# Where the weights of a fused attention and softplus-MoE kernel are converted, and which engine makes its first x tiles

## The chip, the cores and the metric

The kernel runs on one core of a Trainium2 chip. The metric is the device time of one execution in microseconds (us). Five engines work side by side, each through its own instructions in order: TensorE (PE, matmuls; its weight loads are PEld), VectorE (DVE), ScalarE (ACT), GpSimd (POOL) and SyncE (SP), which here issues nearly all DMAs.

## The reference

Attention with rotary embedding over 4 batches of 8 heads (S = 576, D = 64), and its output, laid out as 2304 tokens of 512, through one expert with softplus:

```python
q_rot, k_rot = rotate(q), rotate(k)
scores = (1 / sqrt(D)) * matmul(q_rot, k_rot.T)
scores = scores - max(scores, axis=-1)
attn = exp(scores); attn = attn / (sum(attn, axis=-1) + 1e-9)
x = matmul(attn, v)                      # -> (2304, 512)
h = x @ w_in                             # 512 -> 2048
g = maximum(h, 0) + log1p(exp(-abs(h)))
out = g @ w_out                          # 2048 -> 512
```

## The kernel before

**Precision.** Every matmul runs on pairs of fp32r numbers: an operand is a high part and a low part (the rest), and three products are added. The weights w_in and w_out arrive as 64-bit floats and are turned into such pairs on the chip, by `conv_w`. For one chunk of columns it loads the raw words (`wraw`, L98, SP) and then makes six steps: the upper word scaled on ACT (L115), masked and shifted on DVE (L117) while ACT converts the lower word (L119), the sign merged on DVE (L121), the two added on DVE (L124), the high part wh cast on ACT (L127), the low part wl subtracted on DVE (L129). The generator yields between the steps, so that whoever drives it decides between which other instructions a step stands. The weights of one f (128 of the 2048 inner columns) are 512 columns of w_in and 512 of w_out.

**Attention loop.** It has 160 items, five 128-wide score chunks for each of 32 heads, and 171 slots, s = 0 to 170. In slot s the scores of item s are made on PE (L322) into the one buffer of their kind, and DVE reduces them to a row maximum (mx, L324). Nine slots later the item is made again transposed (L359), ACT takes two exponentials (L365, L366), DVE their difference (pl, L373), and two slots after that PE multiplies with v (pv, L391). `shift1` splits a head's maxima on GpSimd (shl, L270 and L273), and the shift goes into the stacked q. GpSimd also makes most of the rope (L273) and the low part of v (L297). q and k of a head are stacked by DMA (qs, L304 and L305; ks, L306 and L307) out of raw pairs (L260). Finished heads go through `evac` (xt, L399) to DRAM (xd L403, row sums xs L404); when a batch is done, `recip` makes 1/sum on DVE (L413, L414) and writes it to rd.

**MoE.** x comes back from DRAM in tiles of 384 tokens, four chunks of 128 rows each (`load_x`, L154 and L157: one load of xd, two of rd, twice that where a tile reaches over two batches). `split_x` multiplies by 1/sum (L162, GpSimd), rounds to the high part (L165, GpSimd) and subtracts for the low part (L166). There are 96 units, a tile and an f each: `emit_h` makes h (12 matmuls, L173), its softplus through e (DVE L183), ACT L185, m (DVE L188) and the pair g (ACT L190, DVE L193); `emit_o` multiplies with w_out (9 matmuls, L209). h runs two units ahead of o. Units begin with f below SEG for tiles 0 and 1 in turn, then tile 2, then the rest.

**What sets the order.** Nearly all compute instructions are pinned in program order (`pin`, `keep`); DMAs without `pin` are placed by a scheduler. `conv` makes f = 0 and 1 in eight chunks of 256 columns, one step in every third slot from 9 to 159. `late` makes the other f in two generators, w_in and w_out in turn, which `convert` drives: six calls in slots 163 to 168, and then three calls within each unit from the third on; the first six calls drive only the first generator, later ones both, and every sixth call does nothing. x of tiles 0 and 1 is loaded in slots 151 to 158 and split in slots 162 to 169, the low part on DVE. x of tile 2 is loaded and split among the first units.

## Time and profile before

| | |
|---|---|
| runs of the kernel before | median 764.06 us of 3 (762.26 to 764.2) |
| the profiled execution's own time | 763.71 us |
| its span | 761.9 us |
| PE busy | 728.3 us, 96% of the span |
| DVE busy | 520.7 us, 68% |
| ACT busy | 387.2 us, 51% |
| POOL busy | 311.1 us, 41% |
| mean granted clock of PE | 0.982 |

The span runs from the first to the last instruction that the profiler sees. PE is busy nearly throughout. The other engines are much less so, but each of them works beside PE through queues in order, so what matters is the few places where PE waits for one, and a busy PE can hide a short wait, since the ends of its matmuls are modelled.

### The profile page before, as it was taken

To read this page: it belongs to the slowest core of one execution; us is meant where nothing else is said; L and a number is where in the kernel's file an instruction comes from. 1 tells how busy PE (TensorE), PEld (TensorE's weight loads), DVE (VectorE), ACT (ScalarE), POOL (GpSimd) and SP (SyncE) were. 2 spreads that over 40 slices of the span, in tenths; PEclk is the share of its full clock that TensorE was granted. 3 is DMA by queue.
4 is the path that set the end of the run, shared out by engine and by line. 5 is a ranking of instruction groups with operands and counts; after the bars stand their busy time and mean duration, and the time that the engine had idled before them with its cause. 6 is when DMAs were issued, how large, how long until landed. Compare 5 with 4: busy or idle time off the path is not lost.

```text
span 761.9 us, 11924 instructions
## 1 busy us (share of the span) xinstructions
PE 728.3 (96%) x4288; PEld 670.8 (88%) x4288; DVE 520.7 (68%) x812; ACT 387.2 (51%) x730; POOL 311.1 (41%) x376
## 2 busy tenths in 40 slices
PE   5589999999999999998999999999999999999998
PEld 5479999999989999997888989899999989899996
DVE  6468888888888788878988888874353344444343
ACT  1057777777777777675566555532222222222221
POOL 6248888888888888337500000060190000000000
PEclk9589999999999999999999999999999999999999
DMA  6967776877778776743433333232040001001001
GB/s 188 237 154 206 197 206 173 225 196 206 188 204 220 199 189 157 178 142 99 119 108 111 112 111 111 97 118 71 1 145 1 1 1 42 1 1 43 0 1 42
DMA packets 49515, 91.41 MB, mean 120 GB/s; under 512 B 7248, under 2 KB 19856, under 8 KB 49456
## 3 DMA queue, kind: packets, MB, share of 16 engines
q1 hardware_dynamic: 46480, 85.77, 41.8%
q10 hardware_dynamic: 2976, 4.88, 1.7%
q8 instruction: 34, 0.56, 0.3%
q14 instruction: 25, 0.20, 0.1%
HBM read 51.00 MB, written 9.58 MB: 80 GB/s over the span
## 4 chain that ended last, share of the span: by engine, by line
PE 82%; DVE 8%; DMA 4%; issue 2%; POOL 1%; ACT 1%; SPq 1%; POOLq 0%; ACTq 0%; DVEq 0%
PE hp L173 24%; PE pv L391 13%; PE oa L209 12%; PE ob L209 12%; PE sp L322 10%; PE sp L359 10%; DVE mx L324 2%; DMA ks<-raw 2%; DMA qs<-raw 1%; DVE raw L273 1%; DVE pl L373 1%; POOL xraw L162 1%; DMA tab<-cs 1%; DVE g L193 1%; DVE wc L121 1%
## 5 line engine op out<-in xcount | busy, mean ns | idle before, releaser
L173 PE MATMUL hp<-xhl,wh 128*128 128x384 f32 x768 | 196.4, 336 | 0.6 <-DVE m L188 0.6
L324 DVE TENSOR_REDUCE mx<-sp 128x1 f32<-128x576 f32 x160 | 120.9, 755 | 63.5 <-PE sp L322 62.9
L185 ACT ACTIVATE e<-e 128x384 f32<-128x384 f32 x96 | 50.4, 525 | 199.2 <-DVE e L183 189.7
L173 PEld LDWEIGHTS hp<-xhl,wh 128*128 128x128 f32 x768 | 140.5, 188 | 9.5 <-DVE m L188 0.9
L322 PE MATMUL sp<-ks,qs 128*128 128x288 f32 x640 | 119.9, 311 | 22.9 <-DVE mx L324 11.6
L365 ACT ACTIVATE ph<-sp 128x576 fp32r<-128x576 f32 x160 | 103.8, 649 | 59.2 <-PE sp L359 58.9
L173 PE MATMUL hp<-xhl,wl 128*128 128x384 f32 x384 | 129.5, 337 | 0.8 <-DVE wl L129 0.7
L322 PEld LDWEIGHTS sp<-ks,qs 128*128 128x128 f32 x640 | 96.2, 196 | 31.0 <-DVE mx L324 18.7
L359 PE MATMUL sp<-qs,ks 128*128 128x288 f32 x640 | 116.1, 304 | 0.0
L391 PE MATMUL pv<-ph,vs 128*64 128x288 f32 (+1 forms) x640 | 112.2, 297 | 3.0 <-DVE xt L399 2.0
L183 DVE TENSOR_SCALAR e<-hp 128x384 int32<-128x384 int32 x96 | 53.4, 556 | 83.4 <-PE hp L173 83.1
L366 ACT ACTIVATE sp<-sp 128x576 f32<-128x576 f32 x160 | 102.9, 643 | 0.0
L359 PEld LDWEIGHTS sp<-qs,ks 128*128 128x128 f32 x640 | 93.7, 190 | 6.8 <-DVE pl L373 4.7
L209 PE MATMUL oa<-wh,g 128*128 128x512 f32 x288 | 97.7, 393 | 0.0
L373 DVE TENSOR_TENSOR pl<-sp,ph 128x576 fp32r<-128x576 f32 x128 | 95.8, 749 | 2.2 <-ACT sp L366 1.3
L209 PE MATMUL ob<-wh,g 128*128 128x512 f32 x288 | 97.3, 393 | 0.0
L391 PEld LDWEIGHTS pv<-ph,vs 128*64 128x64 f32 (+1 forms) x640 | 84.2, 161 | 5.8 <-ACT ph L365 2.2
L273 POOL TENSOR_TENSOR raw<-raw,tab 128x576 f32<-128x576 f32 x58 | 84.4, 1475 | 9.2 <-DMA raw<-qk 9.2
L193 DVE TENSOR_TENSOR g<-m,g 128x384 fp32r<-128x384 f32 x96 | 59.2, 616 | 37.7 <-ACT g L190 37.4
L273 POOL TENSOR_TENSOR raw<-raw 128x576 f32<-128x576 f32 (+1 forms) x56 | 80.6, 1439 | 3.7 <-ACT raw L267 1.5
L188 DVE SCALAR_TENSOR_TENSOR m<-hp,e 128x384 f32<-128x384 f32 x96 | 53.4, 556 | 41.1 <-ACT e L185 40.4
L190 ACT CAST g<-m 128x384 fp32r<-128x384 f32 x96 | 49.2, 513 | 50.4 <-DVE m L188 46.8
(72 smaller groups left out, 901.7 us busy)
## 6 DMA issues: line engine op xcount, KB each, us to landing
raw<-qk SPq DMA_DIRECT2D x32, 576.0 KB
wraw<-w SPq DMA_DIRECT2D x28, 512.0 KB
ks<-raw SPq DMA_DIRECT2D x32, 320.0 KB
qs<-raw SPq DMA_DIRECT2D x32, 288.0 KB
ks<-raw SPq DMA_DIRECT2D x32, 160.0 KB
vf<-v SPq DMA_DIRECT2D x32, 160.0 KB
qs<-raw SPq DMA_DIRECT2D x32, 144.0 KB
xd<-xt SPq DMA_DIRECT2D x32, 144.0 KB
```

The source lines that it names most:

```text
L173: pin(nc.tensor.matmul(out=hp, lhsT=a[f][:, c * 128:(c + 1) * 128], rhs=pieces[j, c][:, b, :], start=(i == 0), stop=(i == 11),))
L183: pin(nc.vector.tensor_single_scalar(out=e.bitcast(I32), in_=hp.bitcast(I32), scalar=-(2 ** 31), op=ALU.bitwise_or))
L193: pin(nc.vector.tensor_tensor(out=g[:, 1, :], in0=m, in1=g[:, 0, :].bitcast(F32), op=ALU.subtract))
L209: pin(nc.tensor.matmul(out=po, lhsT=g[:, s, t * 128:(t + 1) * 128], rhs=b[f][:, 512:1024], start=(first and i == 0), stop=(last and i == 2),))
L273: pin((nc.vector if e == "V" else nc.gpsimd).tensor_tensor(out=out, in0=in0, in1=in1, op=op))
L322: pin(nc.tensor.matmul(out=sp[:, j, :HS], lhsT=q[:, i, cq], rhs=k[:, 0, ck], start=(i == 0), stop=(i == 1)))
L324: pin(nc.vector.tensor_reduce(out=mx_t[h][:, c:c + 1], in_=sp[:, :, :HS], axis=AX.XY, op=ALU.max, negate=True))
L359: pin(nc.tensor.matmul(out=sp[:, i, :HS], lhsT=k[:, j, ck], rhs=q[:, j, hs], start=(j == 0), stop=(j == 1)))
L365: pin(nc.scalar.activation(out=ph, in_=sp, func=AF.Exp, scale=D ** -0.5))
L366: pin(nc.scalar.activation(out=sp, in_=sp, func=AF.Exp, scale=D ** -0.5))
L373: pin(nc.vector.tensor_tensor(out=pl, in0=sp[:, :, :HS], in1=ph.bitcast(F32), op=ALU.subtract))
L391: pin(nc.tensor.matmul(out=pv[rows, i, :HS], lhsT=lhs, rhs=rhs[:, i, :], start=(c == 0 and j == 0), stop=(c == 4 and j == len(terms) - 1)))
```

## The change

FC goes from 2 to 1: `conv` makes only f = 0, in two chunks of 512 columns, with both loads issued at the very start and its steps in slots 1 to 8. SEG goes from 5 to 4. `late` now begins at f = 1 and is driven in slots 161 to 168, eight calls, and every twelfth call does nothing. In `load_w` a DMA is pinned if n + f is below 2; with f = 1 the first late load of each generator falls under that. x of tiles 0, 1 and 2 is loaded in every second slot from 143 to 165, through a pool of three buffers; `split_x` is a generator, all of it on GpSimd, driven with one or two steps a slot from slot 146 on. The eight reads of x in the first units of MoE are gone. Line numbers after it are lower by one for most of the lines named here (L172 for h, L208 for o, L116 to L130 for the conversion).

```diff
-FC = 2
-SEG = 5
+FC = 1
+SEG = 4
+XS = 146
-    def conv_w(chunks, m, keep):
+    def conv_w(chunks, m, keep, ahead=1):
...
-        load_w(0)
+        for n in range(ahead):
+            load_w(n)
         yield
         for n, (f, i) in enumerate(chunks):
-            load_w(n + 1)
+            load_w(n + ahead)
...
     def load_x(j, c):
-        if j < 2:
+        if j < 3:
             raw = mp["xr"].tile([128, T], F32, tag="xraw", name="xraw")
             rc = mp["xr"].tile([128, T], F32, tag="xrc", name="xrc")
-        elif j == 2:
-            raw, rc = (mp["part"].tile([128, 512], F32, tag="part", name="xpart")[:, :T] for _ in range(2))
...
-    def split_x(j, c, e):
+    def split_x(j, c):
-        pin(nc.gpsimd.tensor_tensor(out=raw, in0=raw, in1=rc, op=ALU.mult))
+        yield pin(nc.gpsimd.tensor_tensor(out=raw, in0=raw, in1=rc, op=ALU.mult))
...
-        pin(e.tensor_tensor(out=t[:, 1, :], in0=raw, in1=t[:, 0, :].bitcast(F32), op=ALU.subtract))
+        yield pin(nc.gpsimd.tensor_tensor(out=t[:, 1, :], in0=raw, in1=t[:, 0, :].bitcast(F32), op=ALU.subtract))
...
+        conv = conv_w([(f, i) for f in range(FC) for i in range(1024 // CW)], CW, pin, 2)
         load_pair(0)
         load_pair(1, (0,))
+        next(conv)
...
-        conv = conv_w([(f, i) for f in range(FC) for i in range(1024 // CM)], CM, pin)
...
-            if 8 < s < NSLOT and s % 3 == 0:
+            if 0 < s < 9:
                 next(conv, None)
+                if s % 2:
+                    next(conv, None)
...
-        if hooks[0] % 6 < 5:
+        if hooks[0] % 12 < 11:
...
-            if NSLOT - 9 <= s < NSLOT - 1:
-                load_x(*divmod(s - NSLOT + 9, 4))
+            if XS - 3 <= s < XS + 21 and (s - XS + 3) % 2 == 0:
+                load_x(*divmod((s - XS + 3) // 2, 4))
+            if s >= XS:
+                for _ in range(1 + s % 2):
+                    next(split, None)
...
-            if s > NSLOT + 1 and s < NSLOT + LAG + 1:
-                split_x(*divmod(s - NSLOT - 2, 4), nc.vector)
-            if NSLOT + 2 < s < NSLOT + LAG:
+            if NSLOT < s < NSLOT + LAG:
                 convert()
...
-    xat = {2 * i: (2, i) for i in range(4)}
+    xat = {}
```

On SP at the start, where the raw pairs are loaded (raw), and q and k of heads 2 and 3 are stacked (qs2, qs3, ks2, ks3), before:

```order
L304 DMA qs3_113<-raw_189 64x576
L305 DMA qs3_113<-raw_189 64x2x576
L306 DMA ks2_108<-raw_231 64x2x640
L306 DMA ks3_109<-raw_231 64x2x640
L260 DMA raw_438<-qk 128x2x576
L307 DMA ks2_108<-raw_231 64x640
L307 DMA ks3_109<-raw_231 64x640
L98 DMA wraw_441<-w 128x256
L98 DMA wraw_942<-w 128x256
```

and after:

```order
L303 DMA qs3_119<-raw_201 64x576
L304 DMA qs3_119<-raw_201 64x2x576
L259 DMA raw_464<-qk 128x2x576
L305 DMA ks2_114<-raw_247 64x2x640
L305 DMA ks3_115<-raw_247 64x2x640
L306 DMA ks2_114<-raw_247 64x640
L306 DMA ks3_115<-raw_247 64x640
```

The load of the next raw pair, which takes the buffer that qs2 and qs3 are copied from, has moved ahead of both copies for ks2 and ks3, and the weight loads have gone from here.

On ACT near the end of the attention loop, the exponentials (L365 and L366 before, L364 and L365 after) and the first late conversion, before:

```order
L366 ACTIVATE sp2_4605<-sp2_4605 128x2x288
L365 ACTIVATE ph_4631<-sp2_4626 128x576
L366 ACTIVATE sp2_4626<-sp2_4626 128x2x288
L365 ACTIVATE ph_4652<-sp2_4647 128x576
L366 ACTIVATE sp2_4647<-sp2_4647 128x2x288
L115 ACTIVATE wc_4671<-wraw_4645 128x512
L365 ACTIVATE ph_4687<-sp2_4682 128x576
```

and after, where ph_4614 belongs to item 154:

```order
L364 ACTIVATE ph_4591<-sp2_4586 128x576
L365 ACTIVATE sp2_4586<-sp2_4586 128x2x288
L116 ACTIVATE wc_4606<-wraw_4584 128x512
L364 ACTIVATE ph_4614<-sp2_4609 128x576
L365 ACTIVATE sp2_4609<-sp2_4609 128x2x288
L120 ACTIVATE wt_4607<-wraw_4584 128x512
```

The first conversion has moved up by two items; before, it read a chunk whose load stood far up in SP's queue.

On SP, where that chunk wraw_4584 now comes from, after (xraw_4576 and xrc_4577 are chunk 9 of x, xt_4537 the head that is written out in slot 160):

```order
L153 DMA xraw_4525<-xd_78 128x384
L156 DMA xrc_4526<-rd_80 64x384 x2
L402 DMA xd_78<-xt_4537 64x576
L403 DMA xs_79<-xt_4537 1x576
L153 DMA xraw_4576<-xd_78 128x384
L156 DMA xrc_4577<-rd_80 64x384 x2
L98 DMA wraw_4584<-w 128x512
L98 DMA wraw_4604<-w 128x512
```

The two pinned weight loads stand behind chunk 9 of x and the write of that head.

On DVE at the start of MoE, units 2 to 4 (e, m and g are a unit's three steps, wc and wl the conversion), before:

```order
L183 TENSOR_SCALAR e_4896<-hp_4883 128x384
L188 SCALAR_TENSOR_TENSOR m_4897<-hp_4883,e_4896 128x384
L129 TENSOR_TENSOR wl2_238<-wc_4671,wh2_237 128x512
L193 TENSOR_TENSOR g_4904<-m_4897,g_4904 128x384
L117 TENSOR_SCALAR wc_4909<-wc_4909 128x512
L183 TENSOR_SCALAR e_4949<-hp_4936 128x384
L117 TENSOR_SCALAR wc_4915<-wc_4915 128x512
L121 SCALAR_TENSOR_TENSOR wc_4909<-wraw_4901,wc_4909 128x512
L188 SCALAR_TENSOR_TENSOR m_4950<-hp_4936,e_4949 128x384
L121 SCALAR_TENSOR_TENSOR wc_4915<-wraw_4669,wc_4915 128x512
L124 ISA wc_4909<-wc_4909,wt_4910 128x1024
L193 TENSOR_TENSOR g_4957<-m_4950,g_4957 128x384
```

and after:

```order
L182 TENSOR_SCALAR e_4875<-hp_4862 128x384
L118 TENSOR_SCALAR wc_4750<-wc_4750 128x512
L118 TENSOR_SCALAR wc_4755<-wc_4755 128x512
L187 SCALAR_TENSOR_TENSOR m_4876<-hp_4862,e_4875 128x384
L122 SCALAR_TENSOR_TENSOR wc_4750<-wraw_4604,wc_4750 128x512
L122 SCALAR_TENSOR_TENSOR wc_4755<-wraw_4720,wc_4755 128x512
L192 TENSOR_TENSOR g_4884<-m_4876,g_4884 128x384
L125 ISA wc_4750<-wc_4750,wt_4751 128x1024
L125 ISA wc_4755<-wc_4755,wt_4756 128x1024
L182 TENSOR_SCALAR e_4916<-hp_4903 128x384
L130 TENSOR_TENSOR wl2_195<-wc_4750,wh2_194 128x512
```

wl2, the low part of w_in of f = 2, stood behind the m of unit 2 and now stands behind the g of unit 3, and the steps of two chunks stand side by side.

## Rows read from the trace of the kernel before

**Rows 1.** The chain that ended last: its share of the span by engine.

```profile
PE 82%; DVE 8%; DMA 4%; issue 2%; POOL 1%; ACT 1%; SPq 1%; POOLq 0%; ACTq 0%; DVEq 0%
```

**Rows 2.** Windows: length, then PE, PEld, DVE, ACT, POOL busy, clock, DMA share, GB/s.

```profile
56.20:329.60 273.40, 268.94 (x1933) 256.06 (x1934) 228.17 (x318) 204.95 (x389) 223.13 (x271) 1.00 0.76 196
329.60:353.61 24.01, 20.63 (x150) 19.64 (x150) 21.00 (x30) 17.91 (x32) 14.92 (x20) 1.00 0.36 96
353.61:758.21 404.60, 403.24 (x2022) 363.65 (x2020) 237.74 (x417) 149.03 (x283) 48.32 (x52) 1.00 0.18 59
...
191.38:200.82 9.44, 9.44 (x70) 9.13 (x71) 7.71 (x12) 7.37 (x16) 8.53 (x12) 1.00 0.71 153
269.43:280.34 10.91, 10.88 (x79) 10.21 (x79) 9.60 (x13) 8.00 (x16) 9.74 (x13) 1.00 0.78 177
```

**Rows 3.** DVE's conversion steps by form: count, busy us, mean ns, idle before.

```profile
L124 DVE CUSTOM_DVE_ANT_0 wc<-wc,wt 128x1024 uint16<-128x1024 uint16 x28 | 20.9, 746 | 0.0
L121 DVE SCALAR_TENSOR_TENSOR wc<-wraw,wc 128x512 int32<-128x512 int32 x28 | 19.7, 704 | 0.0
...
L117 DVE TENSOR_SCALAR wc<-wc 128x512 int32<-128x512 int32 x28 | 12.8, 457 | 0.1
L121 DVE SCALAR_TENSOR_TENSOR wc<-wraw,wc 128x256 int32<-128x256 int32 x8 | 8.7, 1092 | 0.1
```

**Rows 4.** Timeline of a conversion step in the loop, and of PE behind it: start, us.

```profile
278.89 1.52 DVE L124 CUSTOM_DVE_ANT_0 wc<-wc,wt 128x512 uint16<-128x512 uint16 x1
...
281.14 0.79 PE L322 MATMUL sp<-ks,qs 128*128 128x288 f32 x4 [0.40 <-DVE mx L324]
```

**Rows 5.** Timeline of SP and PE, and a window, before slot 10.

```profile
32.27 1.25 SPq L306 DMA_DIRECT2D ks<-raw  x2
...
45.33 0.77 PE L322 MATMUL sp<-ks,qs 128*128 128x288 f32 x4 [1.75 <-DMA ks<-raw]
...
38.14:45.33 7.19, 4.60 (x18) 3.80 (x18) 3.60 (x5) 2.96 (x5) 1.49 (x3) 0.65 0.84 184
```

**Rows 6.** Timelines of POOL, SP, ACT and PE, and a window, end of attention.

```profile
338.05 0.20 POOL L270 TENSOR_SCALAR shl<-mx 128x5 fp32r<-128x5 f32 x1 [1.72 <-DVE mx L324]
...
338.51 1.00 POOL L162 TENSOR_TENSOR xraw<-xraw,xrc 128x384 f32<-128x384 f32 x1
...
338.18 0.58 SPq L154 DMA_DIRECT2D xraw<-xd  x1
338.81 1.08 SPq L157 DMA_DIRECT2D xrc<-rd  x2
...
352.58 0.36 SPq L98 DMA_DIRECT2D wraw<-w  x1
...
342.47 0.65 ACT L365 ACTIVATE ph<-sp 128x576 fp32r<-128x576 f32 x1
...
348.68 0.76 PE L391 MATMUL pv<-ph,vs 128*128 128x288 f32 x4 [2.04 <-DVE xt L399]
...
355.50:356.50 1.00, 1.00 (x9) 0.97 (x8) 0.78 (x1) 0.00 (x0) 0.91 (x2) 1.00 0.60 223
```

**Rows 7.** Timelines of DVE and ACT, and the chain on PE, start of MoE.

```profile
357.31 0.56 DVE L183 TENSOR_SCALAR e<-hp 128x384 int32<-128x384 int32 x1
...
360.74 0.54 DVE L183 TENSOR_SCALAR e<-hp 128x384 int32<-128x384 int32 x1
...
363.54 0.55 DVE L183 TENSOR_SCALAR e<-hp 128x384 int32<-128x384 int32 x1
...
367.81 0.54 DVE L183 TENSOR_SCALAR e<-hp 128x384 int32<-128x384 int32 x1
...
362.52 0.51 ACT L190 CAST g<-m 128x384 fp32r<-128x384 f32 x1 [0.62 <-DVE m L188]
...
364.62 0.60 ACT L127 CAST wh<-wc 128x512 fp32r<-128x512 f32 x1
...
390.16 2.10 PE hp L173 x12
```

More of the change, by code (lines that the diff above doesn't have):

```diff
@@ L39 @@
 PB = 4
-CM = 256
 CW = 512
@@ L64, in rope_attention_softplus_moe @@
     cv_p = pool(ctx, "cv", 3)
-    mp = {"xa": pool(ctx, "xa", 8)}
+    mp = {"xa": pool(ctx, "xa", 8), "xb": pool(ctx, "xb", 4)}
     nc.scalar.preload_act_table_set("natural_log_exp_and_others")
@@ L158, in load_x @@
         xraw[j, c] = raw, rc
-    def split_x(j, c, e):
+    def split_x(j, c):
         raw, rc = xraw.pop((j, c))
-        pin(nc.gpsimd.tensor_tensor(out=raw, in0=raw, in1=rc, op=ALU.mult))
+        yield pin(nc.gpsimd.tensor_tensor(out=raw, in0=raw, in1=rc, op=ALU.mult))
         t = mp["xb" if j % 3 == 2 else "xa"].tile([128, 2, T], F32R, tag="xhl", name="xhl")
         pieces[j, c] = t
-        pin(nc.gpsimd.tensor_scalar(out=t[:, 0, :], in0=raw, scalar1=1.0, scalar2=0.0, op0=ALU.mult, op1=ALU.add))
-        pin(e.tensor_tensor(out=t[:, 1, :], in0=raw, in1=t[:, 0, :].bitcast(F32), op=ALU.subtract))
+        yield pin(nc.gpsimd.tensor_scalar(out=t[:, 0, :], in0=raw, scalar1=1.0, scalar2=0.0, op0=ALU.mult, op1=ALU.add))
+        yield pin(nc.gpsimd.tensor_tensor(out=t[:, 1, :], in0=raw, in1=t[:, 0, :].bitcast(F32), op=ALU.subtract))
     def emit_h(j, f):
@@ L415, in recip @@
             nc.sync.dma_start(out=rd[b].rearrange("h (i n) -> (h i) n", n=S * NH // 128), in_=r)
+        for f in range(FA):
+            alloc_w(f, wa_p)
+        conv = conv_w([(f, i) for f in range(FC) for i in range(1024 // CW)], CW, pin, 2)
         load_pair(0)
         load_pair(1, (0,))
+        next(conv)
         make_identity(nc, ident)
@@ L433, in attention @@
         load_pair(1, (1,))
-        for f in range(FA):
-            alloc_w(f, wa_p)
-        conv = conv_w([(f, i) for f in range(FC) for i in range(1024 // CM)], CM, pin)
         sv = iter(())
@@ L493, in attention @@
                 recip(n3 // (5 * NH) - 1)
-            if 8 < s < NSLOT and s % 3 == 0:
+            if 0 < s < 9:
                 next(conv, None)
-            if s == NSLOT:
+                if s % 2:
+                    next(conv, None)
+            if s == 9:
                 for _ in conv:
@@ L522, in rope_attention_softplus_moe @@
         es_s = es.enter_context(ExitStack())
-        es_x = es.enter_context(ExitStack())
+        mp["xr"] = pool(es, "xr", 3, "right")
         def tail(s):
@@ L527, in tail @@
                 es_r.close()
-                mp["xr"] = pool(es_x, "xr8", 8, "right")
-            if NSLOT - 9 <= s < NSLOT - 1:
-                load_x(*divmod(s - NSLOT + 9, 4))
+            if XS - 3 <= s < XS + 21 and (s - XS + 3) % 2 == 0:
[3 more added lines that the diff above has]
+                    next(split, None)
             if s == NSLOT + LAG - 1:
@@ L542, in tail @@
                 emit_h(*ahead[-1])
+        split = (x for i in range(12) for x in split_x(*divmod(i, 4)))
         recip = attention(es, es_r, es_s, tail)
-        es_x.close()
     wb_p = pool(ctx, "wc", 1)
-    mp["xb"] = pool(ctx, "xb", 4)
     mp["part"] = pool(ctx, "part", 3)
@@ L558, in rope_attention_softplus_moe @@
         if k - 1 in xat:
-            split_x(*xat[k - 1], nc.gpsimd)
+            for _ in split_x(*xat[k - 1]):
+                pass
         if k in xat:
```

## The prediction

> **What bounds the kernel now.** I read the chain of work that ended last first: TensorE (PE) holds 82% of it and VectorE (DVE) 8% [rows 1], so a change off PE counts only where PE waits for it. Then the windows of three stretches: the even part of the attention loop, its end, and the mixture of experts (MoE). Their borders are the start of the maximum (reduce) of slot 15, that of slot 155, and the first h matmul. In the loop, 28 heads of five slots take 273.40 us, 9.764 each; a head into which hardly any stretched conversion falls takes 9.44, and one with two of them 10.91 [rows 2]. PE is shown as busy for 10.88 of that 10.91: matmul ends are modelled, so short waits hide in its busy time, and lengths of heads tell what the gaps don't. In MoE PE is busy for 403.24 of 404.60 us [rows 2]: it has 1.4 us of waits in all, and a unit is an h of 2.10 us [rows 7] and an o of about the same. There is nothing to win there, only to lose.
>
> **Part 1, conversion out of the loop.** Eight chunks of 256 columns go, with four DVE steps each. Such a step should be short, but next to a GpSimd operation it is long: the bit merge takes 1092 ns for 256 columns in the loop and 704 for 512 columns later [rows 3]. The row at 278.89 shows what follows: the sum of one chunk takes 1.52 us, the next reduce waits behind it, and PE stands 0.40 us before its score matmul because the one score buffer isn't free [rows 4]. Without these steps every head should go at the quiet rate, which I set at 9.43 (the quiet heads lie about 9.44): 28 x 9.764 - 28 x 9.43 = 9.4 us. The reciprocals of three batches stay on DVE, and I leave them 0.2. **Term: -9.2**, bounds -7 (a quarter of the excess is GpSimd or the stack's transfers, not conversion) and -10.
>
> **Part 2, two chunks of 512 columns in slots 1 to 8.** Here the granted clock is below full (0.65 in mean from 38.14 to 45.33), slots are longer, and DVE is busy for 3.60 of 7.19 us [rows 5]. The eight DVE steps cost what they cost for 512 columns, 0.46 to 0.75 us [rows 3], one a slot, and fit. What small slips remain fall ahead of the wait before slot 10, 1.75 us for the stacked k [rows 5], which ends on DMA. So this wait decides, and two things move there. Three loads of weights, 256 KB each, leave this stretch for the idle start, a relief. But on SP the load of the next raw pair now stands ahead of the four ks copies, whose first two went at 32.27 before it [rows 5]; it waits for the two q copies. Then 576 KB of raw and 960 KB of ks go together, 1536 KB against 576 + 320 of ks + 512 of weights = 1408 before. At 184 GB/s [rows 5] the 128 KB more are 0.7 us; that the q copies land earlier with 256 KB less ahead of them gives back about 0.5. **Term: +0.2**, bounds -0.5 and +1.5 (the whole 0.7, and 0.8 if the raw goes as late as before).
>
> **Part 3, x of tiles 0 to 2 on GpSimd.** One chunk is a multiply of 1.00 us [rows 6], a rounding and a subtraction that should be no longer: at most 36 us for 12 chunks, over 25 slots of 1.9, 47 us. The rope is done by then, so GpSimd has the room, and DVE loses eight subtractions. Three things stand in queues for it. First, the shift of the last head stood ahead of all x work on GpSimd (338.05 [rows 6]) and now stands behind chunk 6, some 2 us later; most of that lies beside the next item. Second, the loads on SP: one x issue is 0.58, its two reciprocal parts 1.08 [rows 6], so 1.7 a chunk, twice that in tile 1 with its two batches. Third, **the first late weight load (f=1) is now pinned on SP behind the loads of chunk 9**, and ScalarE (ACT) has its conversion in slot 162 ahead of the exponentials of item 154. The arithmetic, in before's times: the copy of slot 160 can't be written out before about 339.4 (1.4 after the shift at 338.05), two issues 1.2, chunk 9 1.7: the weight load issues at 342.3. A load alike issued at 352.58, and bytes still came at 223 GB/s in the window to 356.5 [rows 6], so it lands some 3.4 later: 345.7. ACT's first step takes 0.65: item 154's exponential starts at 346.4 and not at 342.47 [rows 6], 3.9 late. Against that the 2.04 us that PE stood at 348.68 for the xt copy on DVE [rows 6] go, since it stood behind x subtractions on DVE: 3.9 - 2.04 = 1.9. I add 0.3 for the shift. **Term: +2.2**, bounds 0 (the load lands before ACT gets there) and +4.5 (nothing given back, and 0.6 from stretched conversions).
>
> **Part 4, MoE with weights just in time.** Before, w_in of f=2 was ready a unit ahead. Now one segment fewer is ready, and the two converters, which ran out of step, run in step: two steps of each kind stand together on DVE. I walk it from Z, the first h. The starts of e for units 0 to 3 lay at 357.31, 360.74, 363.54 and 367.81, so 3.43, 2.80 and 4.27 apart [rows 7]. With DVE free of x work the first falls at Z + 2.15, the second and third at the same distances. Between the third and fourth now stand the merges in pairs; neighbours overlap by some 0.08, so with the means of [rows 3] this is 2 x 0.38 + 2 x 0.62 + 2 x 0.66 = 3.3 for the pairs and 3 x 0.47 for e, m and g at the 0.55 of an e: 4.7, so e(3) is at Z + 13.1. The cast of wh2 stands on ACT behind unit 3's: from an e to the end of its g cast 360.74 to 363.03, 2.3, plus 0.60 for the cast itself [rows 7], so wh2 is there at Z + 16.0. Unit 4 is the first to want f=2: six pieces of 2.09 and a last pv of 0.5 lie ahead, Z + 13.1. Stall 2.9, and 0.4 more for wl2, which follows: 3.3. The same walk for f=3: e(4) at 19.0, e(5) 4.5 behind it, two merges ahead of its m, wh3 at 27.0; h(6) wants it at 16.9 + 4 x 2.09 = 25.2: 1.8 + 0.4 = 2.2. And o(6) wants the w_out half of f=3, a step later still: 1.7. After that each f has more units and no stall is left. Sum 7.2, less the 1.4 of before, rounded up for the pair of casts: **term +5.9**. Lower bound: e(3) as soon as its h ends (Z + 11.1) gives 0.9 + 0.4 twice and nothing at o(6), 2.5 - 1.4 = +1.1. Upper: the paired merges at 1.52 [rows 4] and not 0.66 add 1.7: +7.6. I keep to the walk, since its durations are rows of this very stretch. The x work of tile 2 that ran in units 0 to 7 on GpSimd hid behind PE and gives nothing.
>
> **Sum.** -9.2 + 0.2 + 2.2 + 5.9 = -0.9 on the profiled execution of 763.71, which is 0.35 below the median of the three runs: 762.8. What a measurement of this kernel can tell from no change is about 0.3%, 2.3 us.
>
> **Rivals.** *Faster, 756.8:* the converters keep up. e(3) comes at its bound, the weight load lands early: -9.2 + 0.2 + 1.0 + 1.1 = -6.9. For it: only the order of the instructions speaks for the stalls, and the walk stacks four waits. Against: the six pieces ahead of unit 4 have a fixed length, and DVE works in order.
> *Slower, 768.6:* SP's queue. The loads of chunk 9 need the buffers of chunk 6 (three are there); if GpSimd is over 0.9 us late with chunk 6, chunk 9's load, the weight load, ACT's step and item 154 are late by as much, one for one. Two slots (3.8) and the 2.04 not given back: 762.8 + 5.8 = 768.6. For it: in-order queues all the way. Against: GpSimd has 1.9 us a slot for one and a half steps of at most 1.0.
> *Shared port, 766.0:* the row at 278.89 shows 1.52 us for a two-input step beside a GpSimd operation [rows 4]. If each of the four conversion steps in slots 162 to 168 is drawn out so from 0.7, they cost 4 x 0.8 = 3.2 more on a DVE that is busy for 21.00 of 24.01 us there [rows 2]: 762.8 + 3.2. The Trainium skill, page "SBUF — State Buffer", section "Who interferes with whom", says that a DVE instruction with two SBUF inputs contends with a GpSimd instruction that reads SBUF, and that the one that issues second blocks outright. By that rule moving x to GpSimd speaks against this change wherever DVE still converts; the trace agrees (1.52 against a mean of 0.75). I give this rival little, because the means of [rows 3] over 28 chunks have steps with x work beside them in them, and one such step in four is all that PE would wait for.
> *It doesn't do what it says, 772:* the long heads come from GpSimd and transfers, so nothing is won in the loop: 762.8 + 9.2.
>
> **How the numbers follow.** Forecast 0.48; faster rival 0.27; SP's queue 0.13; shared port 0.07; no gain in the loop 0.05. The forecast's own spread of some 2 us puts 0.09 below 761.8, 0.03 above 766.4. Faster: 0.27 + 0.09 = 0.36. Slower: 0.03 + 0.10 + 0.02 + 0.05 = 0.20. Same: 0.44. The bounds together reach from -9.4 to +6.7; the range 756.0 to 767.8 leaves out the last rival, about half of SP's queue, and the outer part of the faster case, some 0.2. The likeliest case by itself is 760.5 to 765.5.
>
> **What would show it.** Reduce of slot 15 to that of slot 155 should take 264 us (262.5 to 266.5). From there to the first h 26.2 and not 24.0, with ACT's first late conversion waiting for its DMA. PE's waits in MoE should be about 7 us, at h(4) for wh2, at h(6) for wh3, at o(6) for wl3, and none after unit 8. If heads stay above 9.6 the first term is wrong; if h(4) waits under 1 us the fourth is, and the kernel is clearly faster.

## The result: 768.4 us, slower by 0.55%

The changed kernel takes 768.38 us in the median (767.92 to 770.25, 4 runs) against 764.13 of the kernel before in the same comparison: ratio 1.0055, interval [1.0039, 1.0071]. I had forecast 762.8, no measurable change, with a range to 767.8. So the sign is wrong and the range just misses. The profiled execution took 768.28 us, its span is 766.5.

The windows of the changed kernel, cut as [rows 2] are, with a quiet head in the last row (length, then busy us of PE, its weight loads, DVE, ACT and POOL, granted clock, DMA share, GB/s):

```profile
57.79:321.71 263.92, 263.92 (x1933) 254.99 (x1934) 205.82 (x286) 197.92 (x366) 231.90 (x285) 1.00 0.76 195
321.71:351.28 29.57, 22.10 (x150) 21.27 (x151) 17.96 (x26) 17.99 (x34) 22.66 (x29) 0.94 0.64 176
351.28:762.60 411.32, 405.19 (x2022) 365.01 (x2020) 233.38 (x421) 152.18 (x288) 34.06 (x38) 1.00 0.17 55
200.00:209.43 9.43, 9.43 (x71) 9.11 (x71) 7.29 (x11) 7.07 (x14) 8.07 (x10) 1.00 0.71 206
```

Set against [rows 2], the account closes:

| stretch | before | after | difference | forecast |
|---|---|---|---|---|
| start to the reduce of slot 15 | 56.20 | 57.79 | +1.59 | +0.2 |
| to the reduce of slot 155 | 273.40 | 263.92 | -9.48 | -9.2 |
| to the first h | 24.01 | 29.57 | +5.56 | +2.2 |
| to the end of the last o | 404.60 | 411.32 | +6.72 | +5.9 |
| sum (4.6 between the two executions) | | | +4.4 | -0.9 |

The loop came out as computed: a head now takes 9.43 in the mean, and in the window of 263.92 us PE shows no idle time at all. The whole of it, and more, is lost behind the loop.

At the end of attention PE waits three times. The timeline of the changed kernel there (start, us; in brackets the idle time before and what ended it):

```profile
329.09 1.01 POOL L161 TENSOR_TENSOR xraw<-xraw,xrc 128x384 f32<-128x384 f32 x1 [2.39 <-DMA xrc<-rd]
...
333.20 0.20 POOL L269 TENSOR_SCALAR shl<-mx 128x5 fp32r<-128x5 f32 x1
...
333.74 0.23 PE L341 MATMUL sp<-identr,shl 128*10 128x128 f32 x1 [2.69 <-POOL shl L272]
...
335.06 1.35 SPq L98 DMA_DIRECT2D wraw<-w  x2
...
340.98 0.66 ACT L116 ACTIVATE wc<-wraw 128x512 f32<-128x512 f32 x1 [4.24 <-DMA wraw<-w]
...
343.57 0.75 PE L390 MATMUL pv<-ph,vs 128*64 128x288 f32 x4 [3.21 <-DVE ph L375]
...
346.98 0.76 PE L390 MATMUL pv<-ph,vs 128*128 128x288 f32 x4 [1.57 <-DVE xt L398]
```

GpSimd stands 2.39 us before chunk 6 of x because its loads are late on SP; the last head's shift stands behind that chunk, so PE waits 2.69. The first weight load of f=1 goes out at 335.06, ACT waits for it until 340.98 with the exponentials of item 154 queued behind, and PE waits 3.21. The wait for xt, 2.04 before [rows 6], is still 1.57. In all PE stands idle for 7.47 us of this stretch and not 3.38, which is 4.09 more, and it is busy for 22.10 and not 20.63 with the same 150 matmuls; the 1.47 go with its clock, 0.94 in the mean and not 1.00 (last section).

At the start of MoE, the timelines of DVE, ACT and PE of the changed kernel:

```profile
359.81 0.55 DVE L182 TENSOR_SCALAR e<-hp 128x384 int32<-128x384 int32 x1
...
363.16 1.29 DVE L125 CUSTOM_DVE_ANT_0 wc<-wc,wt 128x1024 uint16<-128x1024 uint16 x2
364.36 0.55 DVE L182 TENSOR_SCALAR e<-hp 128x384 int32<-128x384 int32 x1
...
366.62 1.14 ACT L128 CAST wh<-wc 128x512 fp32r<-128x512 f32 x2
...
367.29 0.62 PE L172 MATMUL hp<-xhl,wh 128*128 128x384 f32 x2 [2.76 <-ACT wh L128]
...
377.87 0.62 PE L172 MATMUL hp<-xhl,wh 128*128 128x384 f32 x2 [1.52 <-ACT wh L128]
...
392.40 0.50 PE L208 MATMUL oa<-wl,g 128*128 128x512 f32 x1 [1.62 <-DVE wl L130]
```

The fourth e, at 364.36, is 4.55 behind the third, where the walk had 4.7, and 13.1 behind the first h at 351.28, the very Z + 13.1 of the walk; the cast of wh2 follows, and h(4), h(6) and o(6) wait at the places that were named, for 2.76, 1.52 and 1.62 us where the walk had 2.9, 1.8 and 1.7.

### The profile page after: what moved, and what is told of

Same layout as the page of the kernel before. It is cut to its first block, busy times and chain, and to the rows that moved or that the text cites. A ratio compares the mean times of both kernels' runs of the same rounds, so it can differ in the third digit from the quotient of the medians.

```text
span 766.5 us, 11897 instructions
## 1 busy us (share of the span) xinstructions
PE 728.4 (95%) x4288; PEld 674.4 (88%) x4288; DVE 496.6 (65%) x788; ACT 386.3 (50%) x718; POOL 314.4 (41%) x384
## 4 chain that ended last, share of the span: by engine, by line
PE 88%; DMA 4%; DVE 4%; ACT 2%; SPq 1%; issue 1%; POOL 1%; DVEq 0%; POOLq 0%; ACTq 0%
PE hp L172 25%; PE pv L390 15%; PE oa L208 13%; PE ob L208 13%; PE sp L358 12%; PE sp L321 10%; DVE raw L272 1%; DMA qs<-shr 1%; DMA qs<-raw 1%; DMA wraw<-w 1%; DMA ks<-raw 1%; DMA tab<-cs 1%; DVE wc L122 0%; ACT raw L266 0%; DMA xrc<-rd 0%
## 5 line engine op out<-in xcount | busy, mean ns | idle before, releaser
L172 PE MATMUL hp<-xhl,wh 128*128 128x384 f32 x768 | 197.0, 337 | 4.3 <-ACT wh L128 4.3
L172 PEld LDWEIGHTS hp<-xhl,wh 128*128 128x128 f32 x768 | 141.0, 188 | 13.2 <-ACT wh L128 5.2
L172 PE MATMUL hp<-xhl,wl 128*128 128x384 f32 x384 | 129.9, 338 | 0.2
L364 ACT ACTIVATE ph<-sp 128x576 fp32r<-128x576 f32 x160 | 103.9, 649 | 51.1 <-PE sp L358 50.9
L365 ACT ACTIVATE sp<-sp 128x576 f32<-128x576 f32 x160 | 102.8, 642 | 0.0
L208 PE MATMUL oa<-wh,g 128*128 128x512 f32 x288 | 98.3, 395 | 0.0
L208 PE MATMUL ob<-wh,g 128*128 128x512 f32 x288 | 97.3, 393 | 0.0
L192 DVE TENSOR_TENSOR g<-m,g 128x384 fp32r<-128x384 f32 x96 | 56.5, 589 | 44.4 <-ACT g L189 44.3
```

The costliest lines, as they stand in the source:

```text
L172: pin(nc.tensor.matmul(out=hp, lhsT=a[f][:, c * 128:(c + 1) * 128], rhs=pieces[j, c][:, b, :], start=(i == 0), stop=(i == 11),))
L192: pin(nc.vector.tensor_tensor(out=g[:, 1, :], in0=m, in1=g[:, 0, :].bitcast(F32), op=ALU.subtract))
L208: pin(nc.tensor.matmul(out=po, lhsT=g[:, s, t * 128:(t + 1) * 128], rhs=b[f][:, 512:1024], start=(first and i == 0), stop=(last and i == 2),))
L364: pin(nc.scalar.activation(out=ph, in_=sp, func=AF.Exp, scale=D ** -0.5))
L365: pin(nc.scalar.activation(out=sp, in_=sp, func=AF.Exp, scale=D ** -0.5))
```

## The experiments

Theory after the result: the loop's gain is real, and it comes from the conversion steps being drawn out beside GpSimd. The loss has three causes of its own: two queue faults at the end of attention (the shift behind chunk 6, the weight load behind chunk 9), and one segment too few converted before MoE. Against it stand: the end is bound by GpSimd's x work as such; MoE loses by x or by DVE being short; the loop pays for the amount of conversion. Each kernel was timed beside the kernel before on the same chip; the medians of before were 764.1 to 766.1.

**The two queues at the end.** e2 issues the first late loads in slot 140:

```diff
+            if s == XS - 6:
+                for x in late:
+                    next(x)
...
-            for x in late[:2 if hooks[0] >= 6 else 1]:
-                next(x, None)
+            for i, x in enumerate(late[:2 if hooks[0] >= 6 else 1]):
+                if hooks[0] != 6 * i:
+                    next(x, None)
```

> The changed kernel, with the first late load of each weight generator issued in slot 140, ahead of all x loads; the conversion steps stand where they stood. Theory: ACT's 4.24 us wait for this load in slot 162 goes, and with it PE's 3.21 us before the product with v at 343.57; PE's 1.57 before the next head's product (xt on DVE) may grow to 2.0. Time from the reduce of slot 155 to the first h: 29.6 to about 26.8; total about 765.6. MoE waits unchanged (2.76, 1.52, 1.62). Rival: the stretch is bound by GpSimd's x chain and the shift, and the gap only moves: under 1 us gained, 767.5 to 768.4.

Measured: 765.8 us (10 runs), ratio 1.003 [1.0006, 1.0053]; the stretch takes 26.88. The waits of PE in it, by what was waited for (us, times, longest):

```profile
PE sp L341 <- POOL shl L272: 3.6, 1, 3.6
PE pv L390 <- DVE xt L398: 1.2, 1, 1.2
```

The wait behind ACT is gone, as the theory had it; the wait for the shift grew from 2.69 to 3.6.

e3 puts the last head's shift ahead of chunk 6 and leaves the weight load where it was:

```diff
-            if s >= XS:
-                for _ in range(1 + s % 2):
+            if s >= XS and s not in (158, 159):
+                for _ in range(1 + s % 2 + (2 if s == 160 else s == 162)):
```

> The changed kernel, with the x steps of slots 158 and 159 put off to slots 160 and 162, so that the shift of the last head stands ahead of chunk 6 on GpSimd. Theory: PE's 2.69 us before the last head's shift fall to under 0.5. But chunk 6 ends later, chunk 9's load waits for its buffer and the weight load behind it goes later too, so ACT's wait for the weights grows by 1 to 2 us: total 767 to 768.5, little gained. Rival: the two waits don't hang together, and the total falls by the whole 2.5 to about 765.8.

Measured: 770.58 us (5 runs, 768.64 to 773.26), ratio 1.0083 [1.0054, 1.0112]. The waits of PE at the end, then the first weight load on SP and ACT's step behind it:

```profile
PE pv L390 <- DVE ph L375: 7.0, 1, 7.0
```

```profile
333.81 1.06 SPq L98 DMA_DIRECT2D wraw<-w  x2
...
339.74 0.67 ACT L116 ACTIVATE wc<-wraw 128x512 f32<-128x512 f32 x1 [6.70 <-DMA wraw<-w]
```

The shift's wait went, and the wait behind ACT grew from 3.2 to 7.0. That is hardly the weight load: it goes out 13.60 behind the reduce of slot 155 (320.21 here) and not 13.35, and ACT has it 5.93 later and not 5.92. Chunk 6 ends 0.24 later on GpSimd, so the loads move with it, one for one as the rival "SP's queue" says, but by a quarter of a microsecond. The rest is PE, which comes to this wait 3.57 us earlier and leaves it 0.26 later: what it no longer loses before the shift, and to the clock behind that wait, it waits out here. So the mend alone gains nothing, and the total is above the 768.5 that I had set as its upper end.

e4 is both edits.

> Both edits together: weights of f=1 loaded early, last head's shift ahead of chunk 6. Theory: both waits of PE (2.69 and 3.21) go, 5.9 us, of which up to 1 comes back at the xt copy: from the reduce of slot 155 to the first h about 24.5 to 25, as before the change (24.0); total about 763.3 to 763.8. Rival (GpSimd's x work is the bound of this stretch): over 26.5 us for the stretch, total over 765.

Measured: 762.21 us (10 runs), ratio 0.9973 [0.9952, 0.9993]. Its windows, end of attention and MoE:

```profile
323.95:346.90 22.95, 20.53 (x151) 19.84 (x152) 17.80 (x27) 17.84 (x34) 18.78 (x24) 1.00 0.57 158
346.90:759.36 412.46, 406.38 (x2022) 366.30 (x2020) 233.25 (x420) 152.22 (x288) 38.07 (x43) 0.99 0.17 55
```

The end is now 22.95, better than the 24.01 of before and than the 24.5 that I had expected: with DVE free of x, GpSimd has room for the x work. So the rival of this stretch falls; the loss there was the two queues, and the clock behind their waits. MoE is no better: it takes 1.14 more than 411.32, and the clock falls twice there where it fell once (last section).

**What a step in the loop costs.** e5 is the kernel before with its steps in other slots; e6 has `(0, 4, 8, 9)` in the same place:

```diff
-            if 8 < s < NSLOT and s % 3 == 0:
+            if s > 9 and s < NSLOT and s % 10 in (1, 2, 5, 7) and s not in (61, 101, 141):
                 next(conv, None)
```

> The kernel before with one edit: the conversion steps of f=0 and f=1 stand in the slots whose number ends in 1, 2, 5 or 7 and not in every third slot (slots 61, 101 and 141 with the reciprocals left out). In the trace of before, steps in such slots cost PE nothing, and those in slots that end in 0, 4, 8 or 9 0.2 to 0.8 us each. Theory 'neighbour': a step is dear only where a GpSimd operation on the shared path stands beside it. Then the stretch from the reduce of slot 15 to that of slot 155 falls from 273.4 to 264 to 265.5, all else stays, total 755 to 756.5. Rival 'amount': the loop pays for the conversion work itself; then the stretch stays at 272 to 274 and the total at 763 to 765.

> The kernel before, the same steps in the slots that end in 0, 4, 8 or 9. Theory 'neighbour': each of the 32 DVE steps is drawn out to 0.9 to 1.5 us and costs some 0.55 in the mean, 18 us: the stretch takes about 282, the total about 773. Rival 'amount': 273 and 764, as before and as with the other slots.

Measured: e5 759.38 us (5 runs), ratio 0.9921 [0.9894, 0.9949]; e6 774.56 (2 runs), ratio 1.0111 [1.0071, 1.0152]. The same instructions, counted by form, in e5:

```profile
L121 DVE SCALAR_TENSOR_TENSOR wc<-wraw,wc 128x256 int32<-128x256 int32 x8 | 6.9, 866 | 0.0
L129 DVE TENSOR_TENSOR wl<-wc,wh 128x256 fp32r<-128x256 f32 x8 | 3.9, 483 | 0.0
L124 DVE CUSTOM_DVE_ANT_0 wc<-wc,wt 128x512 uint16<-128x512 uint16 x8 | 3.8, 477 | 0.0
L117 DVE TENSOR_SCALAR wc<-wc 128x256 int32<-128x256 int32 x8 | 3.6, 450 | 0.0
```

and in e6:

```profile
L121 DVE SCALAR_TENSOR_TENSOR wc<-wraw,wc 128x256 int32<-128x256 int32 x8 | 12.7, 1587 | 0.0
L124 DVE CUSTOM_DVE_ANT_0 wc<-wc,wt 128x512 uint16<-128x512 uint16 x8 | 8.4, 1052 | 0.1
L129 DVE TENSOR_TENSOR wl<-wc,wh 128x256 fp32r<-128x256 f32 x8 | 8.4, 1045 | 0.1
L117 DVE TENSOR_SCALAR wc<-wc 128x256 int32<-128x256 int32 x8 | 7.4, 924 | 0.1
```

Twice as long for the same work. The loop takes in e5 and in e6:

```profile
59.24:324.55 265.31, 264.59 (x1933) 254.87 (x1934) 220.38 (x318) 204.42 (x389) 223.03 (x271) 1.00 0.78 202
```

```profile
57.85:339.39 281.54, 272.61 (x1933) 256.35 (x1934) 237.84 (x319) 205.51 (x389) 222.82 (x271) 1.00 0.74 190
```

265.3 with nothing moved out of it, and 281.5 (282 was expected). Against the 263.9 without any step, the 32 steps cost 1.4 us in one set of slots and 17.6 in the other. e5's total is 3 over the expectation; in its profiled execution that is the start (59.24 to slot 15, 56.20 before) and 1.0 at the end, not the loop. A long step of e6 beside its neighbour:

```profile
128.30 1.65 DVE L121 SCALAR_TENSOR_TENSOR wc<-wraw,wc 128x256 int32<-128x256 int32 x1
...
128.25 1.42 POOL L273 TENSOR_TENSOR raw<-raw 128x576 fp32r<-128x576 f32 x1
```

GpSimd began 0.05 us ahead, for 1.42 us, and DVE's step ends 0.28 behind it. It is so with all: 28 of the 32 steps of e6 begin while a two-input operation of GpSimd runs, and each ends 0.28 us behind that operation (the mask of L117 0.15); the four with none beside them take 0.43. A step lasts as long as what is left of its neighbour.

**Which part loses in MoE.** e7 is the changed kernel with the shift first (as e3) and f=1 converted in the loop's cheap slots; so `late` begins at f=2 as before the change:

```diff
-FC = 1
-SEG = 4
+FC = 2
+SEG = 5
+CM = 256
...
+        conv1 = conv_w([(1, i) for i in range(1024 // CM)], CM, pin)
...
+            if s > 9 and s < NSLOT and s % 10 in (1, 2, 5, 7) and s not in (61, 101, 141):
+                next(conv1, None)
...
-        if hooks[0] % 12 < 11:
+        if hooks[0] % 6 < 5:
```

> The changed kernel with the shift of the last head ahead of chunk 6 (x steps of slots 158 and 159 put off), and with f=1 converted in the loop again, 256 columns at a time, in the slots that end in 1, 2, 5 or 7; so the late generators start at f=2, six calls in slots 163 to 168, every sixth skipped, five segments, as before the change; f=0 stays in slots 1 to 8. Theory: the MoE loss of the change comes from one segment less being ready, not from x or the order of units. Then from the first h to the last o 404.5 to 405.5 and not 411.3, with waits of 1.5 in all; the loop 264 to 265.5; from the reduce of slot 155 to the first h 23 to 24 since the first late load is no longer behind x; total about 756. Rival: tile 2 made early or DVE order keeps PE waiting in MoE: over 408.

Measured: 755.58 us (4 runs), ratio 0.987 [0.9839, 0.9901]. MoE takes 402.25, 2.25 less than the lower end that I had set (e9 shows why), the end 23.00. The loop took 269.46 in the profiled execution (758.36, the slowest of the four), with 2.0 us before a stacked k and 0.9 before a shift, both on DMA; why, I haven't settled.

e8 is the kernel before with e5's slots and with the x part of the change, the shift first; f=0 and f=1 both in the loop, nothing in slots 1 to 8. e9 is e8 with the old slots, so the x part alone.

> The kernel before with the steps in the slots that end in 1, 2, 5 or 7, and in addition the x of tiles 0 to 2 made on GpSimd as in the changed kernel, with the last head's shift ahead of chunk 6; nothing of the conversion in slots 1 to 8. Theory: start as before (reduce of slot 15 at 56 to 57.5), loop 264 to 265.5, end 23 to 24, MoE 404.6: total 753.5 to 755.5, at least 1 below the run with the free slots alone if the end gains. Rival: x on GpSimd gains nothing by itself, total within 0.5 of that run.

> The kernel before with only the x part: x of tiles 0 to 2 on GpSimd from slot 146, the last head's shift ahead of chunk 6; the conversion stays in every third slot. Theory: the x part is worth its own gain, from the first h to the last o 402.3 and not 404.6 (no x work of tile 2 beside the first units, none on DVE ahead of the first e), from the reduce of slot 155 to the first h about 23 and not 24, loop 273 to 274: total 3 to 3.5 below before. Rival: in the run with the free slots these two gains came from the conversion being done earlier; then MoE stays at 404.3 to 404.6 and the total within 1.2 of before.

Measured: e8 754.16 us (4 runs), ratio 0.9853 [0.9817, 0.9889]; e9 760.32 (4 runs), ratio 0.9937 [0.9912, 0.9962]. Windows of e9, loop, end and MoE:

```profile
57.25:330.79 273.54, 268.95 (x1933) 256.06 (x1934) 228.34 (x318) 205.00 (x389) 234.54 (x285) 1.00 0.76 198
330.79:353.45 22.66, 20.58 (x150) 19.66 (x150) 17.71 (x25) 17.30 (x32) 18.47 (x24) 1.00 0.51 139
353.45:755.70 402.25, 402.25 (x2022) 363.92 (x2020) 233.39 (x414) 149.54 (x283) 37.61 (x43) 1.00 0.17 55
```

and of e8, the loop:

```profile
57.09:322.25 265.16, 264.45 (x1933) 254.79 (x1934) 220.43 (x318) 204.56 (x389) 234.26 (x285) 1.00 0.79 205
```

MoE takes 402.24 in e8 too, where I had expected 404.6. So the x part, with the shift put first, gains by itself: 1.35 at the end and 2.35 in MoE, where PE then waits for nothing. 402.25 is the length of MoE without waits; before the change it held 2.35 us of them, of which gaps show 1.4, and the changed kernel holds 9.1. I had called this part's gain nothing.

e10 is e4 with a second call of `convert()` in each of slots 161 to 168.

> The changed kernel with both mends of the end (weights of f=1 loaded early, the last head's shift ahead of chunk 6) and with two calls of the converters in each of the slots 161 to 168 and not one. So w_in of f=2 is ready before the first h. Theory: the MoE waits of the change (2.76 and 1.52 for wh, 1.62 for wl) come from the number of calls before they are wanted; they go, and from the first h to the last o it takes 402.3 to 404 and not 412. DVE has some 9 us more in the end of attention, which grows from 23 to 26 to 29: total 756 to 759. Rival: DVE in MoE is short by itself; then over 406 in MoE.

Measured: 762.0 us (9 runs), ratio 0.9967 [0.9948, 0.9986], where 756 to 759 was expected. MoE falls from 412.46 to 403.09, and no wait for wh or wl is left; the end grows from 22.95 to 30.16, more than the 26 to 29 expected. Its window, and the longest two waits of PE in it:

```profile
324.22:354.38 30.16, 24.21 (x151) 23.01 (x151) 25.00 (x33) 20.33 (x38) 24.37 (x30) 0.83 0.53 155
```

```profile
PE pv L390 <- DVE xt L398: 2.5, 1, 2.5
PE pv L390 <- DVE ph L375: 1.9, 1, 1.9
```

The MoE loss is a matter of how many steps were made ahead, not of DVE being short in MoE. But the end of attention can't take them: it pays back 7.2 of the 9.4, half of it in waits (5.95 idle against 2.42 in e4), mostly for DVE, and half in PE's busy time (24.21 against 20.53), at a mean granted clock of 0.83 and not 1.00.

e11 is e8 with slots 65 and 115 left out:

> The kernel of the run e8_free_x_pool with slots 65 and 115 left out as well, so that no sign merge falls into a slot that ends in 5, the only two steps that were still long there (1.60 and 1.68 us, 0.6 us each in the loop). Theory: loop 264.0 and not 265.2, total about 1.2 below that run, 753. Rival: other steps become the long ones and the loop stays at 265.

Measured: 753.37 us (4 runs), ratio 0.9853 [0.983, 0.9877]; loop 264.68 with 0.56 of a wait on DMA in it. No difference from e8 that can be told.

**The start.** e1 is the changed kernel with the weight loads of f=0 issued behind the second k pair: its `next(conv)` stands behind `load_pair(1, (1,))` and not behind `load_pair(1, (0,))`.

> The changed kernel, with the two 512 KB weight loads of f=0 issued behind the load of the second k pair and not ahead of everything. The changed kernel starts its first scores at 23.23 us, the kernel before at 21.98. Theory 'loads': the megabyte of weights delays the first raw loads; then the first scores go back to about 22.0 and the time falls by 1.2 to about 767.2. Theory 'port': the 1.2 come from the rope of k on DVE (two steps in 3.88 us and not 2.65), which began 0.13 behind a GpSimd operation and was blocked by it; where the weight loads stand changes nothing unless it moves that start, so first scores stay at 23.2, or jump by about 1.2 if the order of the two operations flips. In both, the loads now land near 28 us, so ACT's first conversion step in slot 1 waits for them, and the rope's rounding on ACT behind it may come late: up to +3 us.

Measured: 771.85 us (4 runs, 768.27 to 774.99); first scores at 23.03, no different from the 23.23 of the changed kernel. The two programs were profiled once more:

> The kernel before once more. If the first scores differ between executions of the same program, by whichever of the two engines gets there first, they may start at 22.0 again or at 23.0 to 23.2; if the start is fixed by the program, at 22.0 within 0.1.

> The changed kernel once more. If its later start belongs to the loads that it issues first, the first scores start at 23.2 within 0.1; if it is a matter of the execution, at 21.9 or at 23.2. From the reduce of slot 155 to the first h 29.6, MoE 411.3, loop 264.

Measured, one execution each: the kernel before 763.59 us, first scores at 22.94; the changed kernel 768.16 us, first scores at 23.16, loop 263.97, end 29.27, MoE 411.02. So the 1.25 us between the first scores of the first two traces are no property of the change: the kernel before has them at 21.97 or at 22.94, and with the start of the change they come at 21.93 in e3. The timeline of DVE and GpSimd in the first trace of before (the rope of the first k on DVE, two steps in one row):

```profile
10.45 2.65 DVE L273 TENSOR_TENSOR raw<-raw,tab 128x576 f32<-128x576 f32 x2
10.47 3.89 POOL L273 TENSOR_TENSOR raw<-raw,tab 128x576 f32<-128x576 f32 x2 [3.89 <-DMA raw<-qk]
```

of DVE in its repeat, where GpSimd begins first, at 10.00:

```profile
10.16 3.87 DVE L273 TENSOR_TENSOR raw<-raw,tab 128x576 f32<-128x576 f32 x2
```

and of DVE and GpSimd in the changed kernel:

```profile
10.30 3.88 DVE L272 TENSOR_TENSOR raw<-raw,tab 128x576 f32<-128x576 f32 x2
...
10.17 3.39 POOL L272 TENSOR_TENSOR raw<-raw,tab 128x576 f32<-128x576 f32 x2 [3.58 <-DMA raw<-qk]
```

e12 and e16 take the GpSimd operation away, in the changed kernel and in e1; e13 does so in e11:

```diff
-                e0, e1, e2, e3 = "VVAV" if p == 0 else "VPAV" if p + i == 2 else "PPAP" if p == 1 else "PPPP"
+                e0, e1, e2, e3 = "VVAV" if p == 0 or p + i == 1 else "VPAV" if p + i == 2 else "PPAP" if p == 1 else "PPPP"
```

> The changed kernel with the rope of q of pair 1 on DVE and ACT and no longer on GpSimd, so that no GpSimd operation stands beside the rope of the first k on DVE. Theory 'port': the late first scores (23.2 and not 22.0) come from DVE's rope of k being blocked by a GpSimd operation that began 0.1 ahead of it (3.88 us for two steps that take 1.43 alone). Then these two steps take about 1.5 us, the next one 0.75, and the first scores start at 19.5 to 21, 2 to 3.5 earlier. What of it reaches the end depends on the wait for ks at slot 10; total 765 to 767.5. Rival 'transfers': the first scores wait for ks by DMA whatever DVE does; they stay at 22 to 23.2.

> The kernel of the run e11_best with the same edit to the rope. Theory 'port': first scores at 19.5 to 21, total 1 to 3 below that run: 750.5 to 752.5. Rival: the wait for ks at slot 10 takes it back, 753 to 754.

> The changed kernel with the rope of q of pair 1 on DVE and ACT (as in e12_rope_dve) and with the two weight loads of f=0 issued behind the second k pair (as in e1_loads_later). In e12 DVE's rope of k was no longer blocked, but first scores came at 22.20, in e13, which has the same rope and no early weight loads, at 19.66. Theory 'two locks': the megabyte of weights keeps the DMA engines busy from 8 to 12 us and delays the stack copies, but in the changed kernel this is hidden behind the blocked DVE; then first scores come at 19.5 to 20 here. Rival: the difference is something else in the start; they stay at 22 or later.

Measured: e12 771.19 us (10 runs), e16 769.23 (4 runs), e13 749.53 (4 runs, ratio 0.9804 [0.9769, 0.9839]). The two steps of the rope in e12:

```profile
10.31 1.42 DVE L272 TENSOR_TENSOR raw<-raw,tab 128x576 f32<-128x576 f32 x2
```

The first scores of e12, of e13 and of e16:

```profile
22.20 1.06 PE L321 MATMUL sp<-ks,qs 128*128 128x288 f32 x3 [8.97 <-DMA ks<-raw]
```

```profile
19.66 1.30 PE L322 MATMUL sp<-ks,qs 128*128 128x288 f32 x4 [6.25 <-DMA ks<-raw]
```

```profile
19.92 1.30 PE L321 MATMUL sp<-ks,qs 128*128 128x288 f32 x4 [6.23 <-DMA ks<-raw]
```

From 10 to 12 us, in the windows of e12 (weights loaded first) and of e16 (not):

```profile
10.00:12.00 2.00, 2.00 (x17) 2.00 (x16) 1.97 (x4) 0.00 (x0) 0.00 (x0) 1.00 1.05 366
```

```profile
10.00:12.00 2.00, 2.00 (x18) 2.00 (x17) 1.97 (x4) 0.00 (x0) 0.00 (x0) 1.00 0.53 126
```

There are two locks. With GpSimd away from DVE's side the rope takes 1.42 and not 3.88, but in e12 the first scores still come at 22.20, as its rival had it, since the megabyte of weights holds the DMA engines (share 1.05 against 0.53 in e16, which differs in nothing else); with both edits they come at 19.92. Either edit alone finds the other lock shut: the 0.2 that e1 gained and the 1.0 of e12 lie within what executions with the start of the change differ by (21.93 to 23.26), the 3.3 of both together lie outside. Each is one trace.

The totals of e12 and e16 aren't better. Their start loses most of it again on DVE in slots 2 to 4 (slot 15 at 58.68 and 57.12, against 57.79), and their ends took 31.9 and 33.6, with PE busy for 24.8 and 25.4 us and not 22.10, since the clock falls twice there. The tail that they share with the changed kernel ranged from 29.3 to 33.6 over five traces; why so widely, the runs don't settle. In e13, without those tails, the whole is kept, against e11: 3.57 at the first scores, 3.57 at slot 15, 3.8 in the total. Its 749.53, 1.0 below what was expected, is the fastest version that was run.

## Why the prediction was wrong

**Part 1, right.** -9.2 forecast, -9.48 measured, heads at 9.43. e5 and e6 show the cause as well: the neighbour and not the amount. I had read the drawn-out steps in [rows 3] and [rows 4] correctly, but I took from them only that the steps should leave. They could have been moved by a slot or two.

**Part 2, the step "leave this stretch for the idle start, a relief" failed: +0.2 forecast, +1.59 measured, just beyond its bound.** The start is not idle for DMA: share 1.03 from 10 to 12 us with the weights in it, 0.49 before. How late the first scores come is not what counts: the repeat of before has them 0.97 later than its first trace and reaches slot 15 0.53 earlier. Over all traces the kernels with the start of before (before, its repeat, e9) reach slot 15 at 55.67 to 57.25, those with the start of the change (the changed kernel, its repeat, e2, e3, e4, e10) at 56.46 to 59.90; the middle values are 2.0 apart. So the change costs some 2 us there, though the two groups overlap. The wait for the stacked k before slot 10, which was to decide, is 0.6 to 1.75 in the first three and nothing in three of the other six. What all six have is a conversion step in the way of a reduce on DVE: the sign merge, let fit at 0.70, takes 1.36 us in the changed kernel, and the scores of slot 8 wait 1.28 behind it, against 0.85 in the three of before.

```profile
41.25 1.33 PE L321 MATMUL sp<-ks,qs 128*128 128x288 f32 x4 [1.28 <-DVE mx L323]
```

Four of the six also wait about 1 us for the shift of the first head (1.05 at 43.87 in the changed kernel), which none of the three does.

**Part 3 is the step that turned the sign: +2.2 forecast, +5.56 measured, beyond its bound of 4.5.** Its three queue items were the right ones, but two were mis-sized. The shift was put at 0.3, "most of that lies beside the next item"; it cost 2.69. The 0.3 was right for the steps of chunk 6; the other 2.39 is GpSimd's wait for the loads of chunk 6, which came late on SP and which I had left out. The weight load was issued at 335.06 where the walk says 334.4 (342.3 less the 7.9 by which slot 155 is earlier), but it took 5.9 us to ACT and not 3.4, a figure that no row shows: it ran to the middle of a window in which bytes still came. Two loads of 512 KB went together behind the x chunks, where the row that I scaled from had one; that this is the reason is likely and not tested. And the 2.04 that were to be given back came back as 0.47. Waits make 4.09 of the 5.56; the other 1.47 is PE's clock behind them, which had no place in the sum. e2 to e4 show that nothing else is in this term: with both queues mended it is -1.06 against before.

The rival "SP's queue", at 0.13, came within 0.3 us of the measured time by luck. It put 8.0 on this term, which measured 5.56, and left the others as forecast, which were 1.9 short. Its mechanism, GpSimd late with chunk 6 and the weight load late by as much, made 0.7 us of the 3.8 that it asked for.

**Part 4, right in place; the nearness of its size is in part luck.** +5.9 forecast, +6.72 measured. The three waits came as walked, 2.76, 1.52 and 1.62, for 2.9, 1.8 and 1.7 with the 0.4 for each wl left out. What the sum didn't have are the 1.5 us that PE lost to its clock behind the wait for wh3 (below), and on the other side that before held 2.35 us of waits and not 1.4. Its last sentence was wrong: the x work of tile 2 did not hide behind PE. e9 shows its going to be worth 2.35 in MoE, of which the sum had the 1.4. So moving the weights costs 6.72 + 2.35 = 9.1 there, and the x part repays a quarter of it. Two sums are off by 0.1: the lower bound here is 2.6 - 1.4, and the upper bounds together make +6.6.

**The shared port** took no part in the loss of this change as I had imagined it (steps in slots 162 to 168): its four steps there took 0.43, 1.07, 0.75 and 0.68 us, 0.3 above their means in the trace of before, where the rival had 3.2, and with the queues mended the end is faster than before. It is the cause of the loop's excess, where I did not look for it as a lever. The Trainium skill, page "SBUF — State Buffer", section "Who interferes with whom", says that the issue order decides who blocks. The traces agree: in one and the same program DVE's two steps take 2.65 us where they begin 0.02 ahead of GpSimd's, and 3.87 where they begin 0.16 behind. The 1.52 that the prediction set against a mean of 0.75 is of a step of half that size, which takes 0.43 alone.

**No gain in the loop** is ruled out, and so is the faster rival: its condition, e(3) at the end of its h, did not come about.

## What to carry to other kernels

Before work is moved off a busy loop, look at what it costs by its place in the loop's period: here the same 32 steps cost 1.4 us in one set of slots and 17.6 in another, and moving them within the loop (e5) kept 8.1 of the 9.5 us and lost 1.0 behind the loop, where moving them out lost 12.3. Whoever moves a step to a later stage moves its load too: follow the load through the in-order queue it joins, and ask which in-order engine stands behind its first use. Of two waits in a row, mending the first alone can show nothing, since its time is waited out at the second (e3); mending the second shows (e2, 2.7 us of its stretch). So try such mends together before one is given up.

## What the runs showed of the hardware

A wait of PE costs more than its length where the granted clock falls behind it. The changed kernel in three windows:

```profile
326.00:329.00 3.00, 3.00 (x25) 3.00 (x24) 2.93 (x5) 2.07 (x4) 0.70 (x1) 1.00 0.40 113
335.30:337.70 2.40, 2.40 (x11) 2.37 (x11) 1.69 (x3) 1.23 (x3) 2.23 (x4) 0.50 0.73 164
379.40:382.80 3.40, 3.40 (x11) 3.11 (x11) 0.68 (x2) 0.67 (x2) 0.00 (x0) 0.51 0.00 0
```

Behind the 2.69 us wait for the shift, and again behind the wait for wh3, the granted clock is 0.50, its lower level of 1.2 GHz: 11 matmuls in 2.40 us where 25 took 3.00, which is 1.1 us more, and at 379.40 11 in 3.40 where h makes 12 in 2.10 [rows 7], some 1.5 more. Behind the 2.76 us wait for wh2 it stayed at 1.00 in this execution. That is the rarer case: of the eight traces with this wait, six show the fall at its end, the repeat of the changed kernel among them, and two of these, e4 and e16, show it a second time behind wh3. MoE takes 412.3 to 412.5 in these two; in e3, where one fall lasts twice as long, 412.0; in the other five 411.0 to 411.3. In the ends of e4 and e8, which have no wait above 1.4 us, the clock is 1.00 throughout. I had put no price on this.
